# A list scheduler inside the kernel, TensorE transposes in the head, and gate and value matmuls as two pieces: RWKV-6 attention followed by a SwiGLU feed-forward

## The chip, the cores and the metric

One core of one Trainium2 chip. The metric is the device time of that core in microseconds (us), the median of some runs of the same program on the same inputs. Before the change it was 273.03 us (three runs, 272.2 to 277.14). The profiles are single executions; their spans are 1.7 to 1.9 us shorter than the timed values of the same runs.

## The reference

An RWKV-6 recurrence over 768 tokens for 4 batches and 8 heads of 48 channels, then an RMS norm and a SwiGLU feed-forward layer on all 3072 tokens (384 channels, 1536 hidden).

```python
for t in range(S):                                   # attention, per batch and head
    cur = einsum('bhd,bhe->bhde', u * k_t, v_t)
    y_t = einsum('bhd,bhde->bhe', r_t, state + cur)
    state = w_t[..., None] * state + einsum('bhd,bhe->bhde', k_t, v_t)
# ... y becomes x with shape (3072, 384)
xn  = x / sqrt(mean(x * x) + 1e-6) * rms_g
out = (silu(xn @ w_gate) * (xn @ w_val)) @ w_out
```

## The kernel before

The sequence is cut into six blocks of 128 tokens. A block has four batches, so it is 512 rows for the feed-forward. The attention is written in chunked form: the logarithms of w are summed over the block by matmuls with triangular masks (`cs_mm`), the exponentials of the sums (`cs_exp`) multiply r and k (`r_mul`, `k_mul`), and r and k are then transposed (`rk_tr`) for the score matmuls. Afterwards y becomes x (`x_add`), is normalized (`x_sq`, `x_rstd`, `xn_mul`) and transposed (`xn_tr`), and a gain is multiplied in (`xn_gain`). Then twelve columns of gate and value (`gv_mm`, `silu`, `h_mul`) and four output tiles (`o_mm`, `o_out`) follow. While the feed-forward of block n runs, the attention of block n+1 runs beside it.

```python
def cs_mm(n, j):
    ps = bank["cs", n, j] = psG.tile([128, 1024], FP32, name="ps_g")    # two banks of PSUM
    nc.tensor.matmul(ps[:, 128:512]..., lhsT=mask_lt, rhs=rhs, ...)
    # ... four matmuls into ps[:, 124:128] for the block's total decay
    nc.tensor.matmul(ps[:, 512:896]..., lhsT=mask_nle, rhs=rhs, ...)

def cs_exp(n, j):
    e = ewk[n, j] = pt.tile([128, 4 + 2 * DM], FP32, name="ewk", bufs=5)
    act(LN_EXP, out=e, in_=bank.pop(("cs", n, j))[:, 124:896], func=AF.Exp)

def rk_tr(n, j, eng=None):
    rkT[n, j] = pt.tile([128, 2 * NP, 128], BF16, name="rkT", bufs=5)
    (eng or nc.sync).dma_start_transpose(rkT[n, j], rk[:, n % 2, j]...)

def gv_mm(n, f):
    ps = bank["gv", n, f] = psG.tile([128, 1024], FP32, name="ps_g")
    for half, wt in ((0, wg_sb), (1, wv_sb)):
        for c in range(KC):
            nc.tensor.matmul(ps[:, half * 512:(half + 1) * 512], lhsT=wt[:, c, f * 128:(f + 1) * 128],
                             rhs=xnt[n][:, c, :], start=(c == 0), stop=(c == KC - 1))

def silu(n, f):
    act(SILU, out=sg, in_=bank["gv", n, f][:, 0:512], func=AF.Silu)

def h_mul(n, f):
    nc.vector.tensor_tensor(out=ht[n][:, f, :], in0=bank.pop(("gv", n, f))[:, 512:1024],
                            in1=bank.pop(("sg", n, f)), op=ALU.mult)
# ...
FS, OS = 1.65, 2.6                       # hand-set pace of a column and of an output tile
def slot(n, x): ...                      # a time in the pipeline, T0 = 36
at(slot(m - 1, x) + 0.4, q_copy_o, m, j) # every piece of work gets a time; they are emitted sorted by it
# ...
for i, which in enumerate("wkrv"):       # block 1: one load of four batches for each input
    at(15.0 + i, load, 1, which)
```

Each engine works through its instructions in the order of emission, so the times given by hand are only an order. The Trainium skill, "TensorE: Matmul & The Clock Gate", Part 1, says of the queues of ScalarE and VectorE that they are "strict FIFO".

Of the kernel before, what the change touches and what calls it, by code (L numbers as in the profile page):

```python
# [2 lines left out]

# [6 lines left out]
FP32 = mybir.dt.float32  # L10
# [15 lines left out]
def kernel(  # L26
# [18 lines left out]
    SB = B  # L45
# [8 lines left out]

    const = ctx.enter_context(tc.tile_pool(name="const", bufs=1))
# [18 lines left out]


    plan = []

    def at(time, fn, *args):
        plan.append((time, len(plan), fn, args))


    inp = {}

    def src(t, n, b0, nb):
        return t[b0:b0 + nb, :, n * L:(n + 1) * L, :].rearrange("b h t d -> t (b h) d")

    def load(n, which, b0=0, nb=SB):
        t = {"r": r, "k": k, "v": v, "w": w}[which]
        if (n, which) not in inp:
            inp[n, which] = pin.tile([128, SB, H, D], FP32, name=which + "t")  # L90
        dst = inp[n, which][:, b0:b0 + nb].rearrange("p b h d -> p (b h) d")
        nc.sync.dma_start(out=dst, in_=src(t, n, b0, nb))  # L92
# [24 lines left out]
    nc.vector.memset(mhalf, -0.5)  # L117

# [17 lines left out]
    def load_gv(g):  # L136
        cols = slice(g * FG * 128, (g + 1) * FG * 128)
        for dst, s in ((wg_sb, moe_w_gate), (wv_sb, moe_w_val)):
            nc.gpsimd.dma_start(out=dst[:, :, cols],
                                in_=s[:, cols].rearrange("(c p) f -> p c f", p=128))  # L140

    def load_wo(g):
        nc.gpsimd.dma_start(
            out=wo_sb[:, g * FG:(g + 1) * FG, :],
            in_=moe_w_out[g * FG * 128:(g + 1) * FG * 128, :].rearrange("(c p) m -> p c m", p=128))


    vb, ruk, diag, ydiag, xb, rstd, ewk, rkT, qts = {}, {}, {}, {}, {}, {}, {}, {}, {}
# [6 lines left out]
    def cast_v(n, b0=0, nb=SB):  # L155
        if n not in vb:
            vb[n] = pt.tile([128, SB, H, D], BF16, name="vb")
        nc.scalar.copy(out=vb[n][:, b0:b0 + nb], in_=inp[n, "v"][:, b0:b0 + nb])  # L158

    def ln(n, b0=0, nb=SB):  # L160
        act(LN_EXP, out=lw[:, n % 2, b0:b0 + nb, :, 0:D].rearrange("p b h d -> p (b h) d"),
            in_=inp[n, "w"][:, b0:b0 + nb].rearrange("p b h d -> p (b h) d"), func=AF.Ln)
# [13 lines left out]

    def cs_exp(n, j):
        e = ewk[n, j] = pt.tile([128, 4 + 2 * DM], FP32, name="ewk", bufs=5)
        act(LN_EXP, out=e, in_=bank.pop(("cs", n, j))[:, 124:896], func=AF.Exp)

    def r_mul(n, j):
        nc.vector.tensor_tensor(out=rk[:, n % 2, j, 0, :, 0:D], in0=inp[n, "r"][:, j],  # L182
                                in1=ewk[n, j][:, 4:4 + DM].rearrange("p (h d) -> p h d", h=H), op=ALU.mult)

    def k_mul(n, j, eng):
        eng.tensor_tensor(out=rk[:, n % 2, j, 1, :, 0:D], in0=inp[n, "k"][:, j],  # L186
                          in1=ewk[n, j][:, 4 + DM:4 + 2 * DM].rearrange("p (h d) -> p h d", h=H),
                          op=ALU.mult)

    def bonus_mul(n, j):  # L190
        if n not in ruk:
            ruk[n] = pt.tile([128, SB, H, D], FP32, name="ruk", bufs=1)
            diag[n] = pt.tile([128, SB, H, 1], FP32, name="diag")
            ydiag[n] = pt.tile([128, SB, H, D], FP32, name="ydiag", bufs=2)
        nc.gpsimd.tensor_tensor(out=ruk[n][:, j], in0=inp[n, "r"][:, j], in1=inp[n, "k"][:, j], op=ALU.mult)  # L195
        nc.gpsimd.tensor_tensor(out=ruk[n][:, j], in0=ruk[n][:, j], in1=u_bc, op=ALU.mult)  # L196

    def bonus_sum(n, j):
        nc.vector.tensor_reduce(out=diag[n][:, j].rearrange("p h o -> p (h o)"), in_=ruk[n][:, j],  # L199
                                axis=mybir.AxisListType.X, op=ALU.add)  # L200

    def bonus_v(n, j):
        nc.gpsimd.tensor_tensor(out=ydiag[n][:, j], in0=inp[n, "v"][:, j],  # L203
                                in1=diag[n][:, j].to_broadcast([128, H, D]), op=ALU.mult)

    def rk_tr(n, j, eng=None):
        rkT[n, j] = pt.tile([128, 2 * NP, 128], BF16, name="rkT", bufs=5)
        (eng or nc.sync).dma_start_transpose(rkT[n, j], rk[:, n % 2, j].rearrange("p c h d -> p (c h d)"))

    def q_mm(n, j):  # L210
# [9 lines left out]
        qts[n, j] = pt.tile([128, 2, NP, 128], BF16, name="qts", bufs=3)  # L220

    def q_mask_e(n, j):
        nc.vector.tensor_tensor(out=qts[n, j][:, 0], in0=bank["q", n, j][0],  # L223
                                in1=bc_mid(mask_lt, NP), op=ALU.mult)
# [8 lines left out]
    def st_mm(n, j):  # L233
# [4 lines left out]
        for i in range(NP):  # L238
            nc.tensor.matmul(ps[:, i, :], lhsT=pair(rk[:, n % 2, j, 1], i), rhs=pair(vb[n][:, j], i),
                             start=(n == 0 and i == 0), stop=(i == NP - 1))  # L240

    def st_new(n, j):
        ps, new, wc = bank.pop(("st", n, j)), st[:, (n + 1) % 2, j], ewk[n, j]
# [5 lines left out]
    def y_mm(n, j):  # L249
# [6 lines left out]
        for h in range(H):  # L256
            nc.tensor.matmul(ps[:, h * D:(h + 1) * D], lhsT=q[:, h % 2, h // 2, :],
                             rhs=vb[n][:, j, h, :], start=(n == 0 and h == 0), stop=(h == H - 1))

    def x_add(n, j):  # L260
        xb[n, j] = pt.tile([128, DM], FP32, name="xb", bufs=4)
        nc.vector.tensor_tensor(out=xb[n, j], in0=bank.pop(("y", n, j)),
                                in1=ydiag[n][:, j].rearrange("p h d -> p (h d)"), op=ALU.add)
# [9 lines left out]

    def xn_mul(n, j):
# [3 lines left out]
    def xn_tr(n, j, eng=None):  # L278
        if n not in xnt:
            xnt[n] = pt.tile([128, KC, TS], BF16, name="xnt")  # L280
        (eng or nc.sync).dma_start_transpose(xnt[n][:, :, j * L:(j + 1) * L], bank.pop(("xn", n, j)))
# [6 lines left out]
    def gv_mm(n, f):  # L288
        if n not in ht:
            ht[n] = pt.tile([128, FC, TS], BF16, name="ht", bufs=1)  # L290
        ps = bank["gv", n, f] = psG.tile([128, 1024], FP32, name="ps_g")
        for half, wt in ((0, wg_sb), (1, wv_sb)):
            for c in range(KC):
                nc.tensor.matmul(ps[:, half * 512:(half + 1) * 512], lhsT=wt[:, c, f * 128:(f + 1) * 128],  # L294
                                 rhs=xnt[n][:, c, :], start=(c == 0), stop=(c == KC - 1))

    def silu(n, f):
        sg = bank["sg", n, f] = pt.tile([128, TS], BF16, name="sg", bufs=3)
# [12 lines left out]
    def o_out(n, j):  # L311
# [3 lines left out]
        else:  # L315
            nc.scalar.copy(out=ob, in_=bank.pop(("o", n, j)))
        row0 = j * S + n * L
        nc.sync.dma_start(out=out[row0:row0 + L, :], in_=ob)


    FS, OS = 1.65, 2.6
    P = FC * FS + SB * OS
    T0 = 36.0

    def slot(n, x):

        n, x = n + x // 16, x % 16
        return T0 + n * P + (x * FS if x < FC else FC * FS + (x - FC) * OS)


    for j in range(SB):
        t = 3.0 + 4.0 * j
        for i, which in enumerate("wkrv"):
            at(-10 + 4 * j + i, load, 0, which, j, 1)
        at(t, ln, 0, j, 1)
        at(t + 0.9, cs_mm, 0, j)
        at(t + 1.2, cs_exp, 0, j)
        at(t + 1.6, cast_v, 0, j, 1)
        at(t + 0.5, bonus_mul, 0, j)
        at(t + 2.3, r_mul, 0, j)  # L340
        at(t + 2.4, k_mul, 0, j, nc.vector)
# [132 lines left out]
```

## Time and profile before

| | before |
|---|---|
| profiled span | 270.3 us |
| first gate matmul, blocks 0 to 4 | 53.65, 119.13, 152.76, 183.92, 215.07 us |
| TensorE busy | 192.5 us, 71% of the span |

I call the time from the first gate matmul of block n to that of block n+1 "stage n". Stage 0 took 65.5 us, the stages from 152 us on 31.2 us.

The profile page cuts the span into 40 slices of 6.76 us. Each digit is the busy share of an engine in tenths; PEclk is the clock granted to TensorE.

```profile
PE   0123315286729104969799999999999999999994
...
ACT  2224326723412039765477856967578657524420
...
PEclk9999999999977755999999999999999999999999
DMA  6999999799999998699655999969200850120002
```

From the twenty-first slice (135 us) on TensorE shows nothing but nines until the last slice; before it there are many slices with less than half. The chain of waits, followed back from the last instruction, gives shares of the span by line:

```profile
PE ps_g L294 22%; DMA rkT<-rk 15%; PE ps_q L308 13%; SPq L92 4%; DVE ht L302 3%; PE ps_q L216 3%; DMA xnt<-xn 2%; ACT sg L72 2%; POOL rk L186 2%; DMA wt<-in_w_dram 2%; DMA vt<-in_v_dram 2%; ACT vb L158 2%; POOL ruk L195 2%; POOL ruk L196 2%; DVE rk L186 1%
```

`rkT<-rk` is the transposes of r and k by DMA. The timeline (start, duration, engine, line, operation, output<-input, and in brackets the idle time before it and what ended it) shows the worst wait on ScalarE and what it did to TensorE:

```profile
99.31 1.47 ACT L158 CAST vb<-vt 128x1536 bf16<-128x1536 f32 x1 [13.62 <-DMA vt<-in_v_dram]
...
105.10 0.48 PE L169 MATMUL ps_g<-lw,mask_lt 128*128 128x384 bf16 x1 [16.38 <-ACT lw L72]
```

### The profile page before, as it was taken

To read this page: it belongs to the slowest core of one execution; us is meant where nothing else is said; L and a number is where in the kernel's file an instruction comes from. 1 tells how busy PE (TensorE), PEld (TensorE's weight loads), DVE (VectorE), ACT (ScalarE), POOL (GpSimd) and SP (SyncE) were. 2 spreads that over 40 slices of the span, in tenths; PEclk is the share of its full clock that TensorE was granted. 3 is DMA by queue.
4 is the path that set the end of the run, shared out by engine and by line. 5 is a ranking of instruction groups with operands and counts; after the bars stand their busy time and mean duration, and the time that the engine had idled before them with its cause. 6 is when DMAs were issued, how large, how long until landed. Compare 5 with 4: busy or idle time off the path is not lost.

```text
span 270.3 us, 4039 instructions
## 1 busy us (share of the span) xinstructions
PE 192.5 (71%) x1424; PEld 98.7 (37%) x1424; DVE 139.4 (52%) x247; ACT 137.0 (51%) x234; POOL 133.6 (49%) x183
## 2 busy tenths in 40 slices
PE   0123315286729104969799999999999999999994
PEld 0011103032314002624345445464455444554352
DVE  4442443847523003745875587746786466624430
ACT  2224326723412039765477856967578657524420
POOL 2635743999310206757869568695668713110000
PEclk9999999999977755999999999999999999999999
DMA  6999999799999998699655999969200850120002
GB/s 126 185 200 194 197 209 200 103 168 140 180 129 193 187 180 144 121 206 210 117 117 121 144 229 153 172 147 233 41 17 15 194 96 16 32 102 29 2 29 87
DMA packets 142980, 36.25 MB, mean 134 GB/s; under 512 B 135920, under 2 KB 142960, under 8 KB 142960
## 3 DMA queue, kind: packets, MB, share of 16 engines
q1 hardware_dynamic: 132544, 30.81, 68.4%
q0 software_dynamic: 3984, 3.54, 9.6%
q10 hardware_dynamic: 6432, 1.64, 3.6%
q8 instruction: 11, 0.18, 0.3%
q14 instruction: 9, 0.07, 0.1%
HBM read 26.15 MB, written 4.72 MB: 114 GB/s over the span
## 4 chain that ended last, share of the span: by engine, by line
PE 43%; DMA 21%; POOL 10%; ACT 8%; DVE 8%; SPq 5%; issue 4%; ACTq 0%; DVEq 0%; POOLq 0%
PE ps_g L294 22%; DMA rkT<-rk 15%; PE ps_q L308 13%; SPq L92 4%; DVE ht L302 3%; PE ps_q L216 3%; DMA xnt<-xn 2%; ACT sg L72 2%; POOL rk L186 2%; DMA wt<-in_w_dram 2%; DMA vt<-in_v_dram 2%; ACT vb L158 2%; POOL ruk L195 2%; POOL ruk L196 2%; DVE rk L186 1%
## 5 line engine op out<-in xcount | busy, mean ns | idle before, releaser
L302 DVE TENSOR_TENSOR ht<-ps_g,sg 128x512 bf16<-128x512 f32 x72 | 49.7, 690 | 56.3 <-ACT sg L72 55.7
L72 ACT ACTIVATE sg<-ps_g 128x512 bf16<-128x512 f32 x72 | 42.9, 596 | 53.7 <-PE ps_g L294 53.7
L294 PE MATMUL ps_g<-xnt,wg_sb 128*128 128x512 bf16 x216 | 61.6, 392 | 11.2 <-DVE xnt L284 7.9
L294 PE MATMUL ps_g<-xnt,wv_sb 128*128 128x512 bf16 x216 | 60.4, 389 | 0.0
L308 PE MATMUL ps_q<-wo_sb,ht 128*128 128x384 bf16 x288 | 50.8, 330 | 0.0
L308 PEld LDWEIGHTS <-ht 128*128 128x128 bf16 x288 | 28.4, 99 | 18.5 <-issue 1.4
L169 PE MATMUL ps_g<-lw,mask_lt 128*128 128x384 bf16 x24 | 9.2, 385 | 35.7 <-ACT lw L72 33.9
L294 PEld LDWEIGHTS <-wv_sb 128*128 128x128 bf16 x216 | 21.5, 100 | 28.1 <-issue 4.3
L294 PEld LDWEIGHTS <-wg_sb 128*128 128x128 bf16 x216 | 19.1, 99 | 31.9 <-issue 11.6
L195 POOL TENSOR_TENSOR ruk<-rt,kt 128x384 f32<-128x384 f32 x24 | 24.0, 999 | 13.5 <-DMA rt<-in_r_dram 12.3
L223 DVE TENSOR_TENSOR qts<-ps_q,mask_lt 128x512 bf16<-128x512 f32 x24 | 16.4, 683 | 27.3 <-PE ps_q L218 22.3
L230 POOL TENSOR_SCALAR_AFFINE_SELECT qts<-qts 128x512 bf16<-128x512 bf16 x24 | 16.0, 668 | 27.7 <-ACT qts L227 27.7
L182 DVE TENSOR_TENSOR rk<-rt,ewk 128x384 bf16<-128x384 f32 x24 | 18.2, 762 | 21.0 <-ACT ewk L72 20.9
L271 POOL TENSOR_SCALAR rstd<-rstd 128x1 f32<-128x1 f32 x24 | 5.7, 237 | 46.9 <-ACT junk L267 46.4
L186 POOL TENSOR_TENSOR rk<-kt,ewk 128x384 bf16<-128x384 f32 x20 | 24.1, 1210 | 4.8 <-ACT ewk L72 4.7
L216 PE MATMUL ps_q<-rkT 48*128 48x128 bf16 x96 | 10.6, 239 | 21.9 <-DMA rkT<-rk 21.9
L196 POOL TENSOR_TENSOR ruk<-ruk,u_bc 128x384 f32<-128x384 f32 x24 | 24.4, 1018 | 1.9
L72 ACT ACTIVATE ewk<-ps_g 128x772 f32<-128x772 f32 x24 | 19.4, 813 | 10.1 <-PE ps_g L174 9.8
L203 POOL TENSOR_TENSOR ydiag<-vt,diag 128x384 f32<-128x384 f32 x24 | 19.9, 830 | 6.2 <-DVE diag L199 6.2
L227 ACT CAST qts<-ps_q 128x512 bf16<-128x512 f32 x24 | 13.9, 579 | 15.8 <-PE ps_q L218 13.7
L216 PEld LDWEIGHTS <-rkT 48*128 48x128 bf16 x96 | 6.0, 102 | 32.3 <-DMA rkT<-rk 24.2
L199 DVE TENSOR_REDUCE diag<-ruk 128x8 f32<-128x384 f32 x24 | 13.1, 546 | 8.9 <-POOL ruk L196 8.9
(46 smaller groups left out, 238.4 us busy)
## 6 DMA issues: line engine op xcount, KB each, us to landing
out_dram<-ob SPq DMA_DIRECT2D x24, 192.0 KB, 2.2
wt<-in_w_dram SPq DMA_DIRECT2D x20, 192.0 KB, 4.5
kt<-in_k_dram SPq DMA_DIRECT2D x20, 192.0 KB, 4.7
rt<-in_r_dram SPq DMA_DIRECT2D x20, 192.0 KB, 4.2
vt<-in_v_dram SPq DMA_DIRECT2D x20, 192.0 KB, 3.9
wg_sb<-in_moe_w_gate_dram POOLq DMA_DIRECT2D x3, 384.0 KB, 7.2
wv_sb<-in_moe_w_val_dram POOLq DMA_DIRECT2D x3, 384.0 KB, 9.9
wo_sb<-in_moe_w_out_dram POOLq DMA_DIRECT2D x3, 384.0 KB, 14.7
```

Source lines behind the costliest of these rows:

```text
L72: nc.scalar.activation(**kw)
L182: nc.vector.tensor_tensor(out=rk[:, n % 2, j, 0, :, 0:D], in0=inp[n, "r"][:, j], in1=ewk[n, j][:, 4:4 + DM].rearrange("p (h d) -> p h d", ...
L186: eng.tensor_tensor(out=rk[:, n % 2, j, 1, :, 0:D], in0=inp[n, "k"][:, j], in1=ewk[n, j][:, 4 + DM:4 + 2 * DM].rearrange("p (h d) -> p h d ...
L195: nc.gpsimd.tensor_tensor(out=ruk[n][:, j], in0=inp[n, "r"][:, j], in1=inp[n, "k"][:, j], op=ALU.mult)
L196: nc.gpsimd.tensor_tensor(out=ruk[n][:, j], in0=ruk[n][:, j], in1=u_bc, op=ALU.mult)
L203: nc.gpsimd.tensor_tensor(out=ydiag[n][:, j], in0=inp[n, "v"][:, j], in1=diag[n][:, j].to_broadcast([128, H, D]), op=ALU.mult)
L216: nc.tensor.matmul(qe[:, i, :], lhsT=t[0:D, NP + i, :], rhs=t[0:D, i, :], start=(i == 0), stop=(i == NP - 1))
L223: nc.vector.tensor_tensor(out=qts[n, j][:, 0], in0=bank["q", n, j][0], in1=bc_mid(mask_lt, NP), op=ALU.mult)
L230: nc.gpsimd.affine_select(out=qts[n, j][:, 1], in_=qts[n, j][:, 1], compare_op=ALU.is_gt, fill=0.0, base=0, pattern=[[0, NP], [1, 128]], c ...
L294: nc.tensor.matmul(ps[:, half * 512:(half + 1) * 512], lhsT=wt[:, c, f * 128:(f + 1) * 128], rhs=xnt[n][:, c, :], start=(c == 0), stop=(c ...
L302: nc.vector.tensor_tensor(out=ht[n][:, f, :], in0=bank.pop(("gv", n, f))[:, 512:1024], in1=bank.pop(("sg", n, f)), op=ALU.mult)
L308: nc.tensor.matmul(ps, lhsT=ht[n][:, f, j * L:(j + 1) * L], rhs=wo_sb[:, f, :], start=(f == 0), stop=(f == FC - 1))
```

## The change

The intent: give each piece of work an engine, an assumed duration, what it needs, the buffers it takes and gives back, and a rank. A greedy list scheduler in the kernel's Python then finds one order for all engines. Around it: all r, k, v, w tiles become tiles of one batch with their own rings; r, k and x of blocks 0 and 1 are transposed by TensorE; all k products go to VectorE; exponentials of blocks other than 1 and 2 stay in PSUM; and gate and value are two pieces that other TensorE work can come between.

```diff
+    def rk_pe(n, j):
+        ps = bank["tr", n, j] = psT.tile([128, 2 * NP, 128], BF16, name="ps_t")
+        for c in range(2):
+            for q in range(NP):
+                nc.tensor.transpose(ps[:, c * NP + q, :], pair(rk[:, n % 2, j, c], q), ident)
+    # ... rk_out copies it to SBUF on ScalarE; xn_pe and xn_out do the same for x
-    def gv_mm(n, f):
-        ps = bank["gv", n, f] = psG.tile([128, 1024], FP32, name="ps_g")
-        for half, wt in ((0, wg_sb), (1, wv_sb)):
-            # ... three matmuls into ps[:, half * 512:(half + 1) * 512]
+    def gate_mm(n, f):
+        bank["gv", n, f] = psG.tile([128, 1024], FP32, name="ps_g")   # still one tile of two banks
+        fc_mm(n, f, 0)
+    def val_mm(n, f):
+        fc_mm(n, f, 1)
-    plan.sort(key=lambda e: e[:2])
+    ring = {"w": NIN, "k": NIN, "r": NIN, "v": NIN, ..., "ob": 3, "G": 2, "Q": 2, "T": 2}
+    piece(gate_mm, n, f, "PE", 0.65, R + f, need, takes=[("G", 2)])
+    piece(val_mm, n, f, "PE", 0.65, R + f - 0.5, [(gate_mm, n, f)])
+    piece(silu, n, f, "ACT", 0.62, V + f, need, takes=[("sg", 1)], gives=[("G", n, f, gate_mm)], table=SILU)
+    piece(h_mul, n, f, "DVE", 0.7, V + f, [(silu, n, f), (val_mm, n, f)] + war,
+          gives=[("G", n, f, gate_mm), ("sg", n, f)])
+    # ... some 40 such pieces; loads of block 1 and 2 are tied behind weight loads:
+    behind["w", 1, 0] = ("gv", 0)
+    behind["k", 1, 0] = ("gv", 1)
+    # ... repeatedly take the piece that can start first, by rank among equals:
+    for _, _, p in sorted(order, key=lambda o: o[:2]):
+        p["fn"](p["n"], p["j"], *p["args"])
```

## The prediction

> **What bounds the kernel now.** Two things.
>
> From 119 us to the end, TensorE: in the table of windows it is busy 9.4 to 10.0 of every 10 us between 150 and 260. In the timeline a gate/value column is 6 matmuls in 1.30 us and an output tile 12 in 1.95 us, so a block of 512 tokens needs 12 x 1.30 + 4 x 1.95 = 23.4 us, and the attention of one block beside it 5.9 us (per batch 0.33 + 0.34 + 0.38 + 0.42). Stages of 29.3 us are possible; they take 31.2 us, the last two 27 us.
>
> Before 119 us, waits. The first gate matmul starts at 53.6 us, and the first feed-forward stage takes 65 us. The chain of waits is made of DMA transposes of r and k (15% of the span; median 3.9 us to landing, up to 18.9), loads issued about 1 us apart on the same in-order queue (thirteen from 81 to 94 us), and a v load whose cast (ScalarE idle 13.6 us) holds back a silu and all matmuls from 88 to 105 us. TensorE idles about 40 us before 53 and 32 us from 53 to 119. After idling it runs at half rate: three 512-column matmuls take 1.28 us, not 0.65 (57 and 80 us). The Trainium skill, "TensorE: Matmul & The Clock Gate", Part 1, describes such a gate; the trace agrees.
>
> **What changes.** Blocks 0 and 1 lose their 16 DMA transposes for TensorE transposes and ScalarE copies (estimate from the 0.58 us cast of 512 columns: 1 us for r and k, 0.5 us for x). A batch's chain loses about 5 us of landing twice. ScalarE becomes the head's busiest engine: ln 0.52, exp 0.81, cast 0.5, copies 1.5, square 0.71, scale 0.61, rsqrt about 0.4: 5 us x 4 batches, plus block 1's ln and exp (5.3 us) and a table load (1.28 us) before the first silu. From data at 5 us: first silu near 33 us. The sixteen first loads, 1 us each, end near 19 us and the first weights follow. I take the first gate matmul at 33 us, 20 us earlier.
>
> After it the order and finer rings should keep TensorE fed: stages of 35 (cold clock; block 1's attention and transposes inside), 31, 30.5, 30.5, 28.5, 27 = 182.5 us, plus 3 us of last output, plus 2 us of the timed run above the span. All k products go to VectorE (0.55 us with one operand in PSUM, estimated from undisturbed r products), which takes 24 us from POOL; VectorE stays near 25 us per stage. Splitting gate and value moves little: those matmuls already run back to back.
>
> DMA is the second limit: 0.86 busy until 189 us, about 163 us; minus 16 transposes (about 20 us) some 145 us, barely ahead of need. I add 4 us.
>
> **Predicted: 224 us, range 212 to 240.** Faster 0.95, same 0.04, slower 0.01.
>
> **Right if:** first gate matmul at 30 to 37 us; no DMA transposes in the chain before 60 us; no TensorE gap over 3 us after the first silu; full clock after 45 us; stages near 30 us; TensorE still busy about 192 us.
>
> **Wrong if:** in-order queues stall because true durations differ from the assumed ones (a load stuck behind transposes, a weight piece late at the fifth column): 10 to 20 us more; or ScalarE or VectorE is late in every stage: 2 us each. Lower if the head is ready near 27 us.

## The result, and the profile after

243.47 us (median of four runs, 241.82 to 245.06), against 273.87 us for the kernel before on the same chip (four runs). The ratio of the fast runs is 0.891, with a 95% interval of 0.882 to 0.900. A ratio here is always the mean time of one kernel's fast runs over the mean of the other's fast runs of the same rounds, so it is not quite the ratio of the medians. The direction was right; the size was not, and 243.5 lies outside 212 to 240.

The same rows of the page for the kernel after (slices of 6.0 us):

```profile
PE   0571457899898299997999989899889999999993
...
ACT  2581699385598234867858585475655875224310
...
PEclk9999999999999869999999999999999999999998
DMA  6999999996994677379999999892126220020012
```

Most of TensorE's empty slices at 70 to 105 us are gone, and the full ones begin at about 42 us. But the fourteenth slice (78 to 84 us) still shows a 2, the nineteenth a 7, 8s come up to 180 us, and PEclk drops once more, in the fourteenth and fifteenth slice (78 to 90 us). The chain of waits, by line:

```profile
PE ps_g L340 29%; PE ps_q L364 16%; ACT sg L75 7%; DVE ht L358 6%; SPq L89 3%; DMA wv_sb<-in_moe_w_val_dram 3%; DMA xnt<-xn 2%; DVE rk L202 2%; PE ps_q L246 2%; DVE rk L207 2%; DMA rt<-in_r_dram 2%; DVE xnt L334 2%; DVE st L279 2%; DMA wt<-in_w_dram 1%; PE ps_g L172 1%
```

No transposes of r and k by DMA are left in it. New are `ACT sg` with 7% and `DVE ht` with 6%: before they had 2% and 3%. These are the silu and the product of the feed-forward columns (0.60 and 0.69 us each), which the plan had meant to run beside TensorE's work.

The timelines give the first gate matmul of each block, and with it each stage beside the terms of the prediction. "Rest" is blocks 4 and 5 and the last output.

| us | first gate | stage 0 | stage 1 | stage 2 | stage 3 | rest | span |
|---|---|---|---|---|---|---|---|
| before | 53.7 | 65.5 | 33.6 | 31.2 | 31.2 | 55.2 | 270.3 |
| predicted | 33 | 35 | 31 | 30.5 | 30.5 | 58.5 | 218.5 |
| after | 39.7 | 41.8 | 37.0 | 32.6 | 32.8 | 56.1 | 240.0 |
| difference | +6.7 | +6.8 | +6.0 | +2.1 | +2.3 | -2.4 | +21.5 |

The prediction then added 2 us for the timed run (measured: 1.7 to 1.8) and 4 us for DMA, for which the table has no row: loads that come late lengthen the head and the stages themselves. So what has to be explained are three terms of about 6.5 us each, the head and the first two stages, and 2 us in each later stage. Three readings of the trace of after gave the theories.

**The head.** Every compute engine is idle for at least half of the time between 20 and 30 us, while the DMA engines are busy throughout (share 1.01; windows view: busy time of each engine in that stretch, clock, DMA share, GB/s):

```profile
20.00:30.00 10.00, 2.49 (x30) 1.94 (x29) 2.41 (x6) 4.20 (x10) 4.97 (x7) 1.00 1.01 177
```

The columns after the length are TensorE, its weight loads, VectorE, ScalarE and GpSimd. ScalarE waits in order for casts of v and for a logarithm of block 1, whose loads share the bandwidth with, or are tied behind, the first weights:

```profile
24.35 0.51 ACT L160 CAST vb<-vt 128x384 bf16<-128x384 f32 x1 [3.26 <-DMA vt<-in_v_dram]
25.80 0.52 ACT L75 ACTIVATE lw<-wt 128x384 bf16<-128x384 f32 x1 [0.94 <-DMA wt<-in_w_dram]
...
28.03 0.52 ACT L301 ACTIVATE junk<-xb 128x384 bf16<-128x384 f32 x1
```

The last line is the square of block 0, which the critical path needs; its input had been ready since about 21.7 us.

**The end of stage 0.** TensorE idles 4.0 us before the first gate matmul of block 1, because VectorE does products of block 2 first (from 73 us on three of them take 1.18 to 1.35 us, others 0.55) and then a slow gain:

```profile
77.80 0.46 DVE L199 COPY wcol<-ewk 128x4 f32<-128x4 f32 x1
78.17 0.55 DVE L207 TENSOR_TENSOR rk<-kt,ewk 128x384 bf16<-128x384 f32 x1
78.64 1.34 DVE L202 TENSOR_TENSOR rk<-rt,ewk 128x384 bf16<-128x384 f32 x1
79.91 0.95 DVE L199 COPY wcol<-ewk 128x4 f32<-128x4 f32 x1
80.77 2.72 DVE L334 TENSOR_SCALAR xnt<-xnt,gT 128x512 bf16<-128x512 bf16 x3
...
81.48 0.48 PE L340 MATMUL ps_g<-xnt,wg_sb 128*128 128x512 bf16 x1 [3.97 <-DVE xnt L334]
```

The same three gain multiplications take 0.88 us where nothing disturbs them (at 32.82 us in run 5 below). The Trainium skill, "SBUF — State Buffer", section "Who interferes with whom", says that a VectorE instruction with two inputs in SBUF contends with GpSimd's reads, and that a copy or a scalar multiply in its fast mode can be locked out for the whole length of the other's instruction. The trace agrees: GpSimd runs casts and products through 75.1 to 83.3 us. The products of block 2 have both inputs in SBUF (`kt,ewk`); those of blocks 0 and 3 to 5, with one in PSUM, take 0.548 us on average.

**Every column.** In the last block nothing but the feed-forward runs (weight loads left out):

```profile
214.02 0.81 PE L340 MATMUL ps_g<-xnt,wg_sb 128*128 128x512 bf16 x3
...
214.67 0.81 PE L340 MATMUL ps_g<-xnt,wv_sb 128*128 128x512 bf16 x3
214.91 0.69 DVE L358 TENSOR_TENSOR ht<-ps_g,sg 128x512 bf16<-128x512 f32 x1 [1.24 <-ACT sg L75]
...
215.58 0.60 ACT L75 ACTIVATE sg<-ps_g 128x512 bf16<-128x512 f32 x1 [0.70 <-PE ps_g L340]
215.66 0.81 PE L340 MATMUL ps_g<-xnt,wg_sb 128*128 128x512 bf16 x3 [0.18 <-DVE ht L358]
```

The gate of this column ends at 214.83, but its silu starts at 215.58, right after the last value matmul (215.48). Gate and value are two pieces of the list, but still one tile of PSUM, and the program waits for tiles. The next gate in turn waits for the product that gives the tile back. The view of waits shows the sum of it, for ScalarE and VectorE, and 2.1 us more on the value matmuls, which wait for a silu that reads the other half:

```profile
ACT sg L75 <- PE ps_g L340: 50.9, 53, 4.5
...
DVE ht L358 <- ACT sg L75: 31.0, 41, 1.6
```

### The profile page after: what moved, and what is told of

It is laid out like the page before. It is cut to its first block, busy times and chain, and to the rows that moved or that the text cites. A ratio compares the mean times of both kernels' runs of the same rounds, so it can differ in the third digit from the quotient of the medians.

```text
span 240.0 us, 4241 instructions
## 1 busy us (share of the span) xinstructions
PE 197.6 (82%) x1494; PEld 106.4 (44%) x1512; DVE 151.1 (63%) x296; ACT 138.3 (58%) x262; POOL 109.5 (46%) x163
## 4 chain that ended last, share of the span: by engine, by line
PE 54%; DVE 16%; ACT 13%; DMA 8%; SPq 3%; issue 3%; POOL 1%; DVEq 0%; ACTq 0%; POOLq 0%
PE ps_g L340 29%; PE ps_q L364 16%; ACT sg L75 7%; DVE ht L358 6%; SPq L89 3%; DMA wv_sb<-in_moe_w_val_dram 3%; DMA xnt<-xn 2%; DVE rk L202 2%; PE ps_q L246 2%; DVE rk L207 2%; DMA rt<-in_r_dram 2%; DVE xnt L334 2%; DVE st L279 2%; DMA wt<-in_w_dram 1%; PE ps_g L172 1%
## 5 line engine op out<-in xcount | busy, mean ns | idle before, releaser
L75 ACT ACTIVATE sg<-ps_g 128x512 bf16<-128x512 f32 x72 | 42.9, 597 | 51.4 <-PE ps_g L340 50.9
L340 PE MATMUL ps_g<-xnt,wg_sb 128*128 128x512 bf16 x207 | 60.0, 392 | 8.4 <-DVE xnt L334 5.0
L364 PE MATMUL ps_q<-wo_sb,ht 128*128 128x384 bf16 x288 | 49.1, 326 | 1.3 <-DVE ht L358 1.3
L264 POOL TENSOR_SCALAR_AFFINE_SELECT qts<-qts 128x512 bf16<-128x512 bf16 x16 | 10.1, 635 | 35.0 <-ACT qts L261 35.0
L372 ACT COPY ob<-ps_q 128x384 f32<-128x384 f32 x12 | 5.7, 476 | 22.6 <-PE ps_q L364 22.6
L279 DVE TENSOR_TENSOR st<-ps_t,wcol 48x192 bf16<-48x192 f32 x40 | 14.0, 351 | 4.3 <-PE ps_t L273 3.9
L175 PEld LDWEIGHTS <-lw 128*128 128x128 bf16 x96 | 6.5, 104 | 20.8 <-issue 19.1
L75 ACT ACTIVATE lw<-wt 128x384 bf16<-128x384 f32 x24 | 11.7, 516 | 6.2 <-DMA wt<-in_w_dram 6.2
L315 ACT ACTIVATE xn<-xb,rstd 128x384 bf16<-128x384 f32 x24 | 14.5, 609 | 0.8 <-POOL rstd L306 0.8
L207 DVE TENSOR_TENSOR rk<-kt,ps_g 128x384 bf16<-128x384 f32 x16 | 8.8, 548 | 9.3 <-ACT ps_g L75 9.3
L301 ACT ACTIVATE junk<-xb 128x384 bf16<-128x384 f32 x24 | 12.4, 519 | 3.8 <-DVE xb L296 3.7
```

The lines of the kernel that those rows point to most:

```text
L75: nc.scalar.activation(**kw)
L207: nc.vector.tensor_tensor(out=rk[:, n % 2, j, 1, :, 0:D], in0=inp["k", n, j], in1=bank["cs", n, j][:, 512:896].rearrange("p (h d) -> p h d ...
L279: nc.vector.tensor_tensor(out=new[p0:p0 + D, :, c0:c0 + D], in0=ps[p0:p0 + D, :, c0:c0 + D], in1=wc[p0:p0 + D, 0:NP].to_broadcast([D, NP, ...
L315: nc.scalar.activation(out=xn, in_=xb[n, j], func=AF.Copy, scale=rstd[n, j][:, 1:2])
L340: nc.tensor.matmul(bank["gv", n, f][:, half * 512:(half + 1) * 512], lhsT=(wg_sb, wv_sb)[half][:, c, f * 128:(f + 1) * 128], rhs=xnt[n][:, ...
L364: nc.tensor.matmul(ps, lhsT=ht[n][:, f, j * L:(j + 1) * L], rhs=wo_sb[:, f, :], start=(f == 0), stop=(f == FC - 1))
```

## The experiments

Eighteen kernels ran. All but the one marked gave the right result. Each was timed in rounds beside the kernel before on the same chip. The kernel before varies by up to 3% between runs (268.98 to 277.14 us in these jobs), the changed kernels by one to two, so I give both the median and the ratio, and build on the stage times of the traces where a difference is small. Runs 1 to 4, 5 to 8, 9 to 12, 13 to 16 and 17 and 18 were five jobs, each with its own runs of the kernel before. Across jobs, medians and ratios can tell different sizes, and where they do I say so. A run more than 1.5% above the fastest of the same kernel counts as slow, and only fast runs enter the ratios. In the expectations, letters name theories, and each text says what its letter means.

### 1. Does the splitting of gate and value matter?

```diff
     def gate_mm(n, f):
         fc_mm(n, f, 0)
+        fc_mm(n, f, 1)
     def val_mm(n, f):
-        fc_mm(n, f, 1)
+        pass
-    piece(gate_mm, n, f, "PE", 0.65, ...)
+    piece(gate_mm, n, f, "PE", 1.3, ...)      # and val_mm with 0.0
```

> Gate and value of a column again issued as one piece of 1.3 us, the rest of the change kept (the list scheduler sees the longer piece and orders everything anew). Theory A: the split bought nothing on the chip, because the silu and the value matmuls of one column wait for each other through their common PSUM tile: within 2% of the changed kernel, 239 to 248 us. Theory B: the split is what lets the silu overlap the value matmuls: 72 columns x 0.13 us and more, 250 to 256 us.

Measured: 242.14 us, ratio 0.883 (0.876 to 0.891); after had 243.47 and 0.891. Theory A holds: the split of the change buys nothing.

### 2. The same order with PSUM tiles of one bank each

```diff
-        bank["gv", n, f] = psG.tile([128, 1024], FP32, name="ps_g")
+        bank["gv", n, f] = (psG.tile([128, 512], FP32, name="ps_a"),
+                            psG.tile([128, 512], FP32, name="ps_b"))
     # the cumulative sums likewise; their exponential in two instructions
```

> The order of the changed kernel word for word, but gate and value (and the two halves of the cumulative sum) in two PSUM tiles of one bank each instead of one tile of two banks; the exp becomes two instructions. Theory A (false wait through the common tile): silus start about 0.6 us before the end of the value matmuls, columns in the last block come every 1.30 us and not 1.43 us, waits of value matmuls for a silu vanish: 5 to 9 us less, 234 to 239 us. Theory B (no false wait; the PSUM ring or VectorE sets 1.43 us): no change beyond the 24 x 0.2 us of the longer exps, 243 to 246 us.

Measured: 236.32 us, ratio 0.862 (0.855 to 0.868), 7.2 us less by the medians. In the timeline of the last block (weight loads left out) the gate of a column ends at 213.26, its silu starts at 213.29, while the value matmuls run (until 213.90), and none of the TensorE lines has a wait:

```profile
212.45 0.81 PE L353 MATMUL ps_a<-xnt,wg_sb 128*128 128x512 bf16 x3
...
213.09 0.81 PE L353 MATMUL ps_b<-xnt,wv_sb 128*128 128x512 bf16 x3
...
213.29 0.60 ACT L75 ACTIVATE sg<-ps_a 128x512 bf16<-128x512 f32 x1 [0.70 <-PE ps_a L353]
...
213.74 0.81 PE L353 MATMUL ps_a<-xnt,wg_sb 128*128 128x512 bf16 x3
```

The view of waits shows ScalarE's wait fall from 50.9 to 31.3 us:

```profile
ACT sg L75 <- PE ps_a L353: 31.3, 43, 4.4
```

The Trainium skill, "PSUM — Partial Sum Buffer", section "Summary: rules for kernel authors", says to read PSUM while a matmul runs from a different bank, and its specification table gives a bank 512 float32 values for each partition. The two halves of the old tile were already different banks, so the wait that went was one of the program's own, made by the size of the tile. The result is right with both at once. Theory A stands: in the last block a silu starts every 1.30 and 1.57 us in turn in after, 1.43 on average, and every 1.29 us in run 2. The edit also splits the tile of the cumulative sums; no run separates that part.

### 3. The gain of block 1 ahead of block 2's products

```diff
+    for fn in (k_mul, r_mul, w_tot):
+        move(fn, 2, 2, before=(k_mul, 2, 3))
+    move(x_rstd, 1, 3, before=(bonus_mul, 2, 1))
```

(`move` takes a piece out of the finished order and puts it ahead of another one.)

> Order of the changed kernel with four moves only: the products and the total of block 2, batch 2, behind the gain of block 1 on VectorE, and the rsqrt of block 1, batch 3, ahead of a bonus product on POOL. Theory A (work that is ready queues behind late or long work in an in-order engine, TensorE idles, its clock halves): the first gate matmul of block 1 comes at about 78 us instead of 81.5, the half clock from 81 to 88 us goes, 6 to 8 us less in all, 235.5 to 237.5 us. Rival (capacity: VectorE and ScalarE have too much work in this stage, the wait only moves elsewhere): within 2 us of the changed kernel, 241 to 245 us.

Measured: 242.63 us, ratio 0.884 (0.878 to 0.891): a miss. The gain still starts at 82.43 us in the trace, behind other slow products and copies. Moving one piece of a crowded queue lets the next one stand in the way.

### 4. First weights later, block 1's loads not tied to them

```diff
-    behind["w", 1, 0] = ("gv", 0)
+    move(load_gv, 0, 0, before=(load_gv, 1, 0))
```

> Order of the changed kernel with one move: the first gate and value weights are fetched after the bonus product of the last batch of block 0 instead of before the v loads, and the w loads of block 1 no longer wait for them. Theory A (the weights, slower on the chip than assumed, hold back the v and w loads, and a ScalarE that takes its work in order stands behind the late ln): last v lands near 19.5 us instead of 24.3, first gate matmul near 35.5 us instead of 39.7, 3 to 5 us less, 238 to 241 us. Rival (the bytes are the limit, whoever comes first): v earlier, weights later, first gate matmul at 39 us or later, 242 us or more.

Measured: 240.43 us, ratio 0.877 (0.870 to 0.884). The last cast of v moves from 24.35 to 18.92 us, but the first gate matmul only from 39.72 to 38.14, not to the 35.5 of theory A (the time is inside its range). The gain is the new last link: on VectorE it stands behind a k product of block 1 that waits for its load.

```profile
37.10 0.56 DVE L207 TENSOR_TENSOR rk<-kt,ewk 128x384 bf16<-128x384 f32 x1 [5.70 <-DMA kt<-in_k_dram]
...
37.65 0.87 DVE L334 TENSOR_SCALAR xnt<-xnt,gT 128x512 bf16<-128x512 bf16 x3
```

### 5. That k product behind the second column as well

```diff
+    move(k_mul, 1, 0, before=(gate_mm, 0, 1))      # with run 4
```

> The late weights of e4 plus one more move: the first k product of block 1 goes behind the gain of block 0 on VectorE. In e4 the normalized x was copied by 32.6 us, yet the first gate matmul came at 38.1 us, because the gain stood in VectorE's queue behind a product whose k load was issued only at 31.9 us. Theory A (order, not bandwidth): first gate matmul at 33 to 34.5 us, another 3 to 4.5 us off e4, 236 to 238 us. Rival (weights or block 1's data are then missing, and the time is given back in the first stage): first gate early, but the first gate of block 1 not before 78 us and the whole within 1.5 us of e4, 239 to 242 us.

Measured: 238.76 us, ratio 0.874 (0.869 to 0.879). The first gate matmul comes at 33.87 us, within 0.9 us of the prediction, so 5.8 of the head's 6.7 us can be had by order alone: weights ahead of v, and a product that waits for a load ahead of the gain. But the first gate matmul of block 1 comes at 78.64 us, against 80.33 in run 4: of 4.3 us won, 2.6 are gone within stage 0, which now takes 44.8 us. The time lies between the ranges of theory and rival.

### 6. The products of block 2 with one operand in PSUM

```diff
-            if m in (1, 2):
+            if m == 1:
                 piece(cs_exp_sb, ...)              # exponential copied to SBUF
```

> Block 2's exp is left in PSUM, as for blocks 3 to 5, so that its products read one operand from SBUF and one from PSUM; the list scheduler's order around it is the same but for the banks held longer. Theory A (the lock between VectorE's two-operand products and POOL stretches the queue ahead of the gain of block 1): block 2's products 0.55 us instead of up to 1.35, first gate of block 1 at 79 us or earlier, half clock gone or shorter, 238 to 241 us. Rival (the order alone is at fault): products short, but the first gate of block 1 still at 81 us or later and 242 to 245 us.

Measured: 239.62 us, ratio 0.878 (0.870 to 0.886), 4 us less than after. Stage 0 is 39.0 us. All products of block 2 now take 0.55 us, and TensorE's wait before the gate falls from 3.97 to 1.08 us:

```profile
78.27 0.55 DVE L202 TENSOR_TENSOR rk<-rt,ps_g 128x384 bf16<-128x384 f32 x1
...
79.63 0.38 PE L340 MATMUL ps_g<-xnt,wg_sb 128*128 128x512 bf16 x1 [1.08 <-DVE xnt L334]
```

So the contention of the slow products did cost what the trace suggested; order (run 3) was not the remedy, another place for the operand was. Not all of it is gone: the gain still takes 2.35 us, and TensorE still falls to half clock (0.63 us for one 512-column matmul at 83.22 us).

### 7 and 8. The two large parts of the change apart

Run 7 is the old order with TensorE transposes for blocks 0 and 1; run 8 is the new order with DMA transposes there.

```diff
     def rk_tr(n, j, eng=None):                      # run 7, on the kernel before; xn_tr likewise
+        if n < 2:
+            # ... eight nc.tensor.transpose into a PSUM tile, nc.scalar.copy to rkT
+            return
```

```diff
-            if head:                                # run 8, on the kernel after; for x likewise
+            if False:
                 piece(rk_pe, ...)
```

> The kernel before with one part of the change only: TensorE transposes and ScalarE copies instead of DMA transposes for blocks 0 and 1; its hand-written order is kept. Theory A (the DMA transposes are the wait of the head, whatever the order): first gate matmul at 38 to 43 us instead of 53.6, gaps between 65 and 80 us gone, 252 to 262 us. Rival (the order makes the gain; queues, loads and the late v cast stay): 266 us or more.

> The changed kernel with that part undone: DMA transposes in blocks 0 and 1 too, the list scheduler orders everything anew. Theory A (both parts are needed: the transposes go through the same queue and engines as the loads): 255 to 270 us. Rival (a good order hides the landing of DMA transposes): 243 to 250 us.

Measured: run 7 251.28 us, ratio 0.921 (0.913 to 0.929), first gate matmul at 47.19 us; run 8 270.29 us, ratio 0.990 (0.983 to 0.996), first gate at 48.31 us. Run 7 lies just below theory A's range and run 8 just above it; run 7's first gate comes 4 us later than expected. Of the 30 us of the change, the transposes alone bring 22, the rest alone 3. The new order is worth something only when the transposes no longer go through the DMA queue.

### 9. Less work for VectorE in stage 0

VectorE is busy 31.8 of the 40 us from 40 to 80 in after. Run 9 is run 6 with half of block 1's masks on ScalarE and GpSimd, as later blocks have it.

```diff
-            if head:
+            if m == 0:
                 piece(q_mask_ov, ..., "DVE", ...)    # else q_copy_o on ScalarE, q_mask_o on GpSimd
```

> As run six (the exponentials of block 2 stay in PSUM), and half of the causal masks of block 1 (four of eight) go from VectorE to a ScalarE copy and a GpSimd select, as the later blocks have it. Theory V: stage 0 is paced by what VectorE has to do (31.8 us busy of the 40 us from 40 to 80 in the trace of the changed kernel), so 4 x 0.4 us of it less give a time of 236 to 238.5 us, and the first gate matmul of block 1 comes 38 us or less after that of block 0 (39.0 in run six). Rival P: stage 0 is paced by TensorE's own work, the false waits and the half clock; then the time stays at 239 to 241 us and the stage at 39 us.

Measured: 242.14 us with two of four runs slow; the ratio of the fast runs is 0.888 (0.876 to 0.901). Stage 0 is 41.2 us. It isn't faster than run 6. Theory V, that VectorE's load paces stage 0, fails here.

### 10. Both PSUM edits, and the list told of two rings

```diff
-            piece(gate_mm, ..., takes=[("G", 2)])
-            piece(val_mm, ..., [(gate_mm, n, f)])
+            piece(gate_mm, ..., takes=[("GA", 1)])
+            piece(val_mm, ..., [(gate_mm, n, f)], takes=[("GB", 1)])
-            piece(silu, ..., gives=[("G", n, f, gate_mm)], ...)
+            piece(silu, ..., gives=[("GA", n, f, gate_mm)], ...)
     # h_mul gives ("GB", n, f, val_mm); with the edits of runs 2 and 6
```

> Runs two and six together (gate and value in PSUM tiles of their own, the exponentials of block 2 in PSUM), and the scheduler is told that the two tiles are two rings, a gate tile being free after silu and a value tile after the product. If the gains of the two runs are independent (7 and 4 us): 231 to 233.5 us. If what the list knows of the rings matters too (a gate matmul may start before the product of two columns ago): 227 to 231 us. If both gains are the same VectorE time of stage 0 told twice: 235 to 237 us.

Measured: 231.69 us (231.58 to 234.5), ratio 0.860 (0.851 to 0.870). By the medians runs 2 and 6 saved 7.2 and 3.9 us, and together 11.8, as if they were independent and the rings in the list added less than 1 us. By the ratios of their three jobs it is 8.0, 3.5 and 8.3 us, each uncertain by 3 us or more, and by the spans of the profiles 5.6, 2.8 and 10.1. So that the two gains add up fully is likely and not shown. From block 2 on this kernel has the stages that the prediction wanted: 31.1, 29.9, rest 53.7 us. The head (41.2) and stage 0 (40.0) are as they were.

### 11. Run 10 with less work for VectorE

The edit of run 9 on run 10.

> Run ten with the masks of run nine. Theory V (VectorE paces stages 0 and 1): 1.5 to 3 us under run ten. Rival P: the same as run ten within 1 us.

Measured: 231.97 us, ratio 0.858 (0.849 to 0.867). The same. Theory V fails a second time, for the whole. But in the trace stage 0 is shorter, 37.2 us against 40.0 in run 10 (the first gate of block 1 at 78.42 instead of 81.22), and 1.3 us of these 2.8 are left at the end. VectorE's load does count in stage 0; the gain is mostly given back later.

### 12. Run 10 with the better head

```diff
     # run 10 and run 5, and:
-    behind["k", 1, 0] = ("gv", 1)
+    behind["k", 1, 0] = ("gv", 0)
```

> Run ten with the head of run five (first gate and value weights issued late, the loads of w for block 1 no longer behind them, the first k product of block 1 after the first column) and the first load of k for block 1 behind the first weights and not the second, so that the queue of loads doesn't stand still. Run five won 5.8 us at the first gate matmul and lost all but 1.7 us of it by the start of block 1. If that loss was late k data and crowded VectorE that the relief of run ten ends, this run is 4 to 6 us under run ten, first gate at 33 to 35 us. If stage 0 is paced by work that the order cannot move (VectorE), it is 1 to 2 us under it, and stage 0 is longer by what the head is shorter.

Measured: 228.46 us (226.5 to 229.81), ratio 0.844 (0.835 to 0.854). The first gate matmul comes at 33.09 us, 8 us earlier than in run 10, but the first of block 1 at 78.08, only 3 us earlier. Stage 0 has grown from 40.0 to 45.0 us. Expected was a gain of either 4 to 6 or 1 to 2 us; 3.2 lies between. GpSimd held three reciprocal roots of block 1 behind a product of block 2 whose r load came late (3.58 us), and the transposes wait for the roots:

```profile
65.23 0.99 POOL L226 TENSOR_TENSOR ruk<-rt,kt 128x384 f32<-128x384 f32 x1 [3.58 <-DMA rt<-in_r_dram]
66.30 0.99 POOL L227 TENSOR_TENSOR ruk<-ruk,u_bc 128x384 f32<-128x384 f32 x1
67.38 0.19 POOL L318 TENSOR_SCALAR rstd<-rstd 128x1 f32<-128x1 f32 x1
...
68.91 0.34 PE L339 MATMUL ps_t<-ident,xn 128*128 128x128 bf16 x3 [1.65 <-ACT xn L328]
```

### 13 to 15. Three waits taken away one after the other

```diff
+    move(bonus_mul, 2, 0, before=(bonus_v, 2, 0))            # run 13, on run 12
+    move(bonus_sum, 2, 0, before=(bonus_v, 2, 0))
```

```diff
+    for j in (0, 1, 2):                                      # run 14, on run 13
+        move(k_mul, 1, j, before=(k_mul, 1, 3))
```

Run 15 is run 14 with the edit of run 9 (and the order that the list then finds).

> Run twelve with one move on GpSimd: the bonus product of block 2, batch 0, which waited for its r load from 61.6 to 65.2 us, comes behind the reciprocal roots of batches 1 to 3 of block 1 and no longer ahead of them (its sum on VectorE moves with it). Theory G (the in-order GpSimd queue holds the end of stage 0): the normalized x of batch 1 comes 3 us earlier, TensorE's 1.65 and 2.93 us waits before the transposes and the first gate matmul go or shrink, output tile 3 runs at full clock: first gate of block 1 at 73.5 to 75.5 us instead of 78.1, time 224.5 to 226.5 us. Rival D (VectorE's products of block 2, which free the cumulative sums' PSUM, hold it): gate at 77 us or later and 228 us.

> Run thirteen with the k products of block 1 (which wait for DMA until 37.4 to 39.2 us in run twelve's trace) behind the first two products h, which stood behind them. Theory Q: TensorE's wait from column 2 to 3 (about 3 us around 38 to 40 us) goes, and 1.5 to 3 us of it remain at the end. Rival V (VectorE's work of stage 0 is dense from 40 to 58 us and takes the same time whichever comes first): within 0.7 us of run thirteen.

> Run fourteen with half of block 1's masks on ScalarE and GpSimd. With the early head VectorE is 9.6 to 10.0 us busy of 10 between 40 and 60 us, so if its load paces stage 0 now: 1 to 2.5 us under run fourteen. If not: the same within 0.7 us, as runs ten and eleven were.

Measured: 228.47, 229.51 and 228.83 us; ratios 0.837 (0.829 to 0.845), 0.842 (0.835 to 0.848), 0.839 (0.833 to 0.846). None is faster than run 12 by its median, so the gains expected of runs 13 and 14 did not come, and run 15 is within 0.7 us of run 14, as for "if not". The first gate matmul of block 1 stays at 78.55 (profiled in a slow run), 78.38 and 76.27 us. The waits of runs 13 and 14 did go: TensorE waits no longer before the transposes, and from 30 to 40 us it is busy for 8.85 us in run 14 against 7.07 in run 13. In run 14 the output tiles of block 0 are done at 69.1 us and the cumulative sums of block 2 at 71.9 us, and then:

```profile
73.94 0.48 ACT L386 COPY ob<-ps_q 128x384 f32<-128x384 f32 x1 [5.82 <-DMA out_dram<-ob]
...
78.38 0.61 PE L353 MATMUL ps_a<-xnt,wg_sb 128*128 128x512 bf16 x1 [6.48 <-DVE wcol L212]
```

ScalarE stands 5.8 us (4.8 of them after the tile to be copied is ready) for a free output buffer, and behind it, in order, stand the last transposed copy of block 1 and the exponentials of block 2. The buffers are late because the stores are issued on the same in-order queue as the loads of block 2:

```profile
62.75 3.68 SPq L89 DMA_DIRECT2D rt<-in_r_dram  x4
66.55 3.73 SPq L89 DMA_DIRECT2D vt<-in_v_dram  x4
70.37 1.42 SPq L391 DMA_DIRECT2D out_dram<-ob  x2
```

### 16. No weight traffic at all (wrong result)

Run 10 with the three weight tiles filled by a constant. It was to bound what the shared DMA bandwidth costs.

```diff
+    nc.gpsimd.memset(wg_sb..., 0.01)                # wv_sb and wo_sb likewise
     def load_gv(g, _):
-        ...
+        pass                                        # load_wo likewise; no load tied to a weight load
```

> Wrong result on purpose: run ten without any weight load (the three weight tiles are filled with a constant at the start, and the loads that were tied to a weight load are no longer tied). 3.5 MB of transfers go. Theory B (shared DMA bandwidth makes the loads of blocks 0 to 2 late, the forecast's second limit): first gate matmul at 34 us or before instead of 41.2, first gate of block 1 at 70 to 74 instead of 81.2, time 219 to 225 us. Rival O (order and engines hold the head and stage 0): first gate at 38 us or later, time 228 us or more. Filling the weights takes GpSimd some us at the start, which may delay the constants that it makes there.

Measured: 228.28 us against run 10's 231.69 (both medians, in different jobs); ratio 0.833 (0.822 to 0.845) against 0.860; the first gate matmul at 38.42 instead of 41.24, that of block 1 at 76.21 instead of 81.22. By these numbers rival O holds, but narrowly, and its test of the head is spoilt. The edit put new work where it took work away: GpSimd fills the weight tiles from 2.33 to 14.02 us, so its first product comes at 13.99 us instead of 7.31 in run 10, and VectorE, in order, stands 7.68 us behind it:

```profile
10.08 3.94 POOL L140 MEMSET wo_sb<- 128x4608 bf16 x1
13.99 0.99 POOL L225 TENSOR_TENSOR ruk<-rt,kt 128x384 f32<-128x384 f32 x1
...
16.08 0.55 DVE L230 TENSOR_REDUCE diag<-ruk 128x8 f32<-128x384 f32 x1 [7.68 <-POOL ruk L226]
```

So the 3.4 us between the medians (7.4 by the ratios) are no upper bound of what the bandwidth costs, and what it costs in the head stays open. Stage 0 is another matter. All loads of blocks 0 to 2 had been issued by 47 us, and the DMA engines stood still afterwards (windows view; the last three columns are clock, DMA share and GB/s):

```profile
50.00:60.00 10.00, 9.84 (x79) 4.70 (x79) 8.86 (x15) 6.03 (x12) 3.23 (x4) 1.00 0.00 1
```

The timeline still has the wait:

```profile
76.21 0.61 PE L352 MATMUL ps_a<-xnt,wg_sb 128*128 128x512 bf16 x1 [3.32 <-DVE wcol L211]
```

Even with nothing left to load, stage 0 takes 37.8 us, 2.2 less than in run 10, so bandwidth isn't what holds its second half. What the trace shows before 76.21 is a serial chain: the last output tile and the cumulative sums of block 2's batches 2 and 3 (TensorE, until 72.9), their exponentials (ScalarE, until 74.0), then gain, a bonus sum and products (VectorE, until 76.1), which give the PSUM tile back that the gate needs.

### 17 and 18. The output buffer, and the next wait

```diff
-        ob = pt.tile([128, DM], FP32, name="ob", bufs=3)
+        ob = pt.tile([128, DM], FP32, name="ob", bufs=4)     # run 17, on run 14
```

Run 18 is run 15 with this buffer, and with block 2's products and the gain ahead of state updates and bonus sums on VectorE.

> Run fourteen with a fourth output buffer and nothing else. Theory S (the stores held by the queue of loads hold ScalarE, and with it the exponentials of block 2 and the last transposed copy of block 1): ScalarE's 4.7 us wait goes, TensorE's wait of 6.5 us before the first gate matmul of block 1 falls to 2 to 3 us, gate at 74 to 75 us instead of 78.4, time 225 to 227 us against 229.5. Rival C (another wait takes its place at once, as in the runs before): gate at 77 us or later, time 228.5 us or more.

> Run fifteen with the fourth output buffer, and on VectorE at the end of stage 0 the products of block 2 and the gain ahead of the state updates and the bonus sums (which wait for GpSimd). If order alone held stage 0: the first gate matmul of block 1 at 72.5 to 74 us instead of 76.3, 223.5 to 225.5 us, about the forecast's 224. If the wait moves on again: 227 us or more.

Measured: run 17 227.34 us (226.2 to 229.01), ratio 0.834 (0.826 to 0.842); run 18 227.55 us (six runs, 226.53 to 229.78), ratio 0.832 (0.825 to 0.840). Run 17's gate comes at 75.79 us instead of 78.38 and the time falls by 2.2 us: the buffer's wait was real, but more than half of it found a successor. (The two kernels ran in different jobs, the intervals of their ratios overlap, and gate and time lie just outside theory S, far from rival C.) Run 18 puts the gate at 72.75 us, as expected, and is still no faster: the wait moves on. Its TensorE timeline shows where it goes:

```profile
72.75 0.82 PE L353 MATMUL ps_a<-xnt,wg_sb 128*128 128x512 bf16 x2 [1.52 <-DVE wcol L212]
75.31 0.48 PE L283 MATMUL ps_t<-st,ident 128*128 128x384 bf16 x1 [1.74 <-DVE st L292]
...
77.33 0.28 PE L259 MATMUL ps_q<-rkT 48*128 48x128 bf16 x1 [1.21 <-DMA rkT<-rk]
...
78.49 1.48 PE L353 MATMUL ps_b<-xnt,wv_sb 128*128 128x512 bf16 x3
```

The state updates that stepped aside are now awaited, then block 2's transposed r and k, and after these waits TensorE is at half clock (1.48 instead of 0.81). The gate came 3 us earlier and the column after it did not.

The stage table of the kernels that matter:

| us | first gate | stage 0 | stage 1 | stage 2 | stage 3 | rest | span |
|---|---|---|---|---|---|---|---|
| after | 39.7 | 41.8 | 37.0 | 32.6 | 32.8 | 56.1 | 240.0 |
| run 2 | 41.0 | 40.5 | 36.0 | 33.1 | 30.3 | 53.7 | 234.4 |
| run 5 | 33.9 | 44.8 | 37.1 | 32.6 | 32.8 | 56.1 | 237.2 |
| run 10 | 41.2 | 40.0 | 33.9 | 31.1 | 29.9 | 53.7 | 229.9 |
| run 12 | 33.1 | 45.0 | 31.3 | 31.6 | 29.9 | 53.7 | 224.7 |
| run 16 (no weights) | 38.4 | 37.8 | 33.1 | 34.3 | 29.9 | 53.5 | 226.9 |
| run 17 | 33.7 | 42.1 | 34.2 | 31.6 | 29.9 | 53.8 | 225.3 |
| run 18 | 33.0 | 39.8 | 37.3 | 32.2 | 31.2 | 53.7 | 227.2 |

Runs 12, 17 and 18 start block 2 between 109.4 and 110.0 us, however the 76 us before are divided (runs 14 and 15, not in the table, at 112.8 and 110.9). Each row is one execution, and that of run 12 was its fastest, 2 us below its median, while that of run 18 was 1.5 us above its own. Runs 12, 17 and 18 all beat both kernels; run 17 has the lowest median and needs only the small edits named above.

## Why the prediction was wrong, point by point

**The direction and the main mechanism were right.** TensorE transposes took the DMA transposes out of the chain of waits, as the prediction said, and run 7 shows that they alone bring 22 of the 30 us.

**The step that failed first: "After it the order and finer rings should keep TensorE fed: stages of 35 ..., 31, 30.5, 30.5".** They were 41.8, 37.0, 32.6 and 32.8 us: 17.2 us more in four terms. I took two pieces in the list for two pieces on the chip. Gate and value stayed one tile with one wait, and the products of block 2 kept both operands in SBUF. Run 10, with both repaired, is 11.8 us faster than after by the medians (runs 2 and 6 show the parts, 7.2 us by tiles of one bank and 3.9 us by the operand in PSUM; by the ratios 8.3, 8.0 and 3.5). In its trace the four stages lose 9.3 us and the rest 2.4, and stages 2 and 3 are 31.1 and 29.9 us, as predicted. I read "those matmuls already run back to back" off the timeline of before, which was right about the matmuls but said nothing of who waits for them. The loss was already there: in the last block of before the gates of two successive columns start 1.57 and 1.30 us apart in turn (at 249.06, 250.63 and 251.93 us), so a column took 1.43 us and not the 1.30 of the sum, though the page shows nothing but nines. "Splitting gate and value moves little" thus came true (run 1) for a reason that I hadn't seen. The list's promise was visible in the diff: silu and product both give back the same "G" of the gate.

**The second: "I take the first gate matmul at 33 us".** It came at 39.7. The 33 us were possible: runs 5 and 12 reach 33.9 and 33.1 without moving fewer bytes. The sum was of ScalarE's work and left out what stands ahead of it in order: the first weights compete with the last v loads and hold back block 1's w loads, and a k product stands ahead of the gain. This is what "Wrong if" named ("a load stuck behind transposes", "true durations differ from the assumed ones"), but the range allowed it too little. Repairing it gave 3.2 us on run 10, not 8, because stage 0 grew.

**"All k products go to VectorE (0.55 us with one operand in PSUM ...)".** Right for the sixteen that have the operand in PSUM (0.548 us), wrong for blocks 1 and 2, whose exponentials go to SBUF: 0.663 us on average for k and 0.894 us for r, and up to 1.35. "VectorE stays near 25 us per stage" was wrong for stage 0 (31.8 us in 40 us). Runs 9 and 11 say that this load alone doesn't set the time: taking work off VectorE shortened stage 0 by 2.8 us in the trace of run 11, and the whole not measurably.

**"DMA is the second limit ... I add 4 us".** Not decided. Without any weight traffic the time falls by 3.4 us by the medians and 7.4 by the ratios (run 16, against run 10, in another job), and that run lost time in the head to the filling of the tiles. Late loads are part of the head's loss (v at 24.35 us, with the DMA engines busy throughout). The last stages, where DMA is mostly idle, were 2.4 us shorter than predicted, so no 4 us came there.

**The signs named in advance.** No DMA transposes before 60 us: right. First gate at 30 to 37 us, no TensorE gap over 3 us, full clock after 45 us: wrong (39.7 us, 4.0 us, half clock from 81 to 88 us). TensorE busy about 192 us: 197.6.

**What stays open.** By the medians, from 243.5 us the PSUM edits lead to 231.7 (11.8 us), the head's order to 228.5 (3.2), the moves of GpSimd's and VectorE's work and the output buffer to 227.3 (1.1, which is within the noise). To 224 there are 3.3 us left, and stages 0 and 1 still take 76 us instead of 66. It is shown that neither the share of VectorE's load that was moved (9, 11) nor one single wait (13, 14, 15, 17, 18) is the cause by itself, and that the end of stage 0 waits even with the DMA engines idle (16). No run took the weight traffic away with the order of run 12 and without the filling, so bandwidth in the head and the start of stage 0 is a rival left open. Of the waits, each that was taken away was followed by another within a few us. That these blocks are bound by a web of in-order queues which no single move can loosen is the reading that fits all of this, but I have not shown an order that does without the waits, so it is argued and not shown.

## What to carry to other kernels

Two pieces of a schedule are two pieces only if what they wait for and give back are separate too: look at the tiles (here two banks in one tile), and read who waits for whom, not only whether the busy engine is dense. A list scheduler with guessed durations is cheap to correct with the trace: find the one instruction in an in-order queue that waits for a load and see what useful work stands behind it. When an experiment takes work away, see that it puts none in its place: the fill of run 16 held the very engine that the head needed. And when a repair of the head is given back in the next stage, compare the start times of later stages before trying the next repair, and put operands where engines don't contend before changing order.

## What the Trainium skill lacked or had wrong

- "ScalarE: Activation LUTs", "What ACT_TABLE_LOAD costs": it gives about 1283 ns for the load and about 1380 ns of drain beside it, 2.66 us for a switch. The load is right (1283 ns in each of ten in after), but in run 18 a load starts 0.02 us after the end of the last exponential (72.34), at 72.36 us, and the silu starts at 73.65 us: 1.3 us in all, no further drain.
- "TensorE: Matmul & The Clock Gate", section "Why this matters for your kernels", asks for no idle gaps over about 3 us. In run 15 shorter ones, of 2.29, 1.16 and 0.70 us with 0.6 to 0.8 us of small matmuls between them, were enough for half clock (0.61 us for one 512-column matmul at 76.27 us, against 0.38 us for one in run 6 at 79.63).
- The same page, Part 4, gives about 275 ns for one 128x128 transpose in a kernel. Single ones agree (260 and 267 ns on average in after), but it doesn't say that they overlap: eight transposes take 0.62 us from the first start to the last end in runs 5 and 18, slower ones 1.03 to 1.06 us. That transposes don't count as work for the clock, as the part says, fits the trace of run 15 but isn't shown by it: after 3.2 us in which TensorE waited (1.39 and 0.65 us) or transposed (41.3 to 44.5 us) three matmuls take 1.49 us.
- "SBUF — State Buffer", "Who interferes with whom", quotes slowdowns of 6.8 times for VectorE and 1.5 times for GpSimd but no operation or duration with them: here 0.55 us becomes up to 1.35 us for a product with both inputs in SBUF, and three gain multiplications of 0.88 us become up to 2.72 us.
- No page says that a program's wait is for a whole tile, so that a tile of two banks joins work that the banks would let overlap: 7.2 us in run 2 by the medians.
